# First pair's q and k loaded as f32 by SyncE and cast on chip; batch 0's masks added by VectorE

## The chip, the cores and the metric

The kernel runs on one core of a Trainium2 chip. The metric is the device time of one execution in microseconds (us), the median of several runs. Engines: PE (TensorE, matmuls), DVE (VectorE), ACT (ScalarE), POOL (GpSimd) and SP (SyncE, which here only issues DMAs). Each engine works through its own instruction list in order, and they wait for each other through semaphores.

## The reference

Sliding-window causal attention for 8 batches of 8 heads, 576 positions, head size 64, window 64; its output, as 4608 tokens of 512 features, goes through a two-layer network with the activation h cos(h).

```python
scores = scale * np.matmul(q, k.transpose(0, 1, 3, 2))      # scale = 1 / 8
rel = pos[:, None] - pos[None, :]
scores = np.where((rel >= 0) & (rel < 64), scores, -1000000000.0)
scores = scores - np.max(scores, axis=-1, keepdims=True)
attn = np.exp(scores)
attn = attn / (np.sum(attn, axis=-1, keepdims=True) + 1e-09)
x = np.matmul(attn, v)                       # then (B, H, S, D) -> (B*S, H*D)
h = x @ w_in                                 # 512 -> 2048
out = (h * np.cos(h)) @ w_out                # 2048 -> 512
```

## The kernel before, in words

**Units and groups.** A unit is 64 query positions of one batch and of one pair of heads, with the 128 key positions that they can see. Its scores are a tile of 128 x 128: 64 queries of each of the two heads on the partitions, 128 keys along the row. Four units make a group, which fills one PSUM bank (128 x 512 f32). Batch 0's first eight query blocks of the four pairs make eight groups, called (pair).(half) below; they are handled ahead of everything else.

**The first stage.** The string FIRST writes out the order of the first stage by hand. Each step emits the instructions of one piece of work, and as each engine works in order, the string sets the order on all of them. The steps: tq and tk transpose a pair's q and k on PE (18 transposes of 64 x 64 each, L186) into PSUM; pq and pk copy the result to SBUF, on DVE (d) or ACT (a); mk makes the masks; s is a group's scores on PE; m its maximum; e its four exponentials with their sums on ACT (L288); i the reciprocals on DVE; n the normalization (L302) on POOL (p) or DVE; w transposes the result on PE (L311) and c copies it; z spreads values of v; v is the product with the values on PE (L330), x its copy into xT; l issues the next weight or batch-1 load on POOL; tb loads ACT's sine table; h are the first matmuls of the first layer (L351). Behind the string the first token tile's dense matmuls run (L351, then L522), and batch 1's attention is placed between them by a list of due times, counted in groups of dense matmuls of PE.

**Loads.** All loads from memory are issued by POOL, which converts f32 to bf16 in the transfer: a pair of batch 0 (load_heads, 128 x 576) q and k apart, pair 0 first, then pairs 1, 2 and 3, the values, the weights and batch 1. The first issue on POOL stands behind the making of the identity matrix (masks.py), and the number ramp for the masks (iota, L115) stands behind the first two. SP issues nothing before 45 us.

**Masks.** From the ramp five DVE operations (L119 to L123) make three 128 x 128 f32 masks: 0 where a key may be seen, about -8e9 where not. Three ACT casts (L125) make a bf16 copy in the order that a group needs.

**Scores of batch 0** (g_scores). One matmul with the identity as weights writes a group's masks into the bank (L238, 128 x 512), and eight matmuls of 64 x 64 x 128 add the scores (L244). q had been multiplied by the scale when it was copied (L197, L199). g_max then takes the negated maximum of each of the four units with one reduction on DVE (L273), and the exponentials read the scores straight from PSUM.

**Scores of later batches** (burst). No mask matmul; for each unit one DVE operation (L277) adds the mask to the scores, multiplies by minus the scale, writes the result s to SBUF and yields the minimum of each row as the exponential's bias; a second instruction reads that minimum out. The exponentials read s, with scale -1.

Of the kernel before, what the change touches and what calls it, by code (L numbers as in the profile page):

```python
# [22 lines left out]
BIG = 3.0e38  # L23
# [28 lines left out]
def kernel(  # L52
# [34 lines left out]
    mask = const.tile([128, 3, 128], F32, name="mask")  # L87
    mask16 = const.tile([128, 6, 128], BF16, name="mask16")

# [28 lines left out]
    def put_masks():  # L118
        nc.vector.tensor_tensor(out=mask[:, 2], in0=mask[:, 0], in1=mask[:, 0], op=ALU.mult)  # L119
        nc.vector.tensor_scalar(mask[:, 1], mask[:, 2], 64.0 ** 2, NEG, ALU.is_gt, ALU.mult)  # L120
        nc.vector.tensor_scalar(mask[:, 2], mask[:, 1], -1.0, NEG, ALU.mult, ALU.add)
        nc.vector.tensor_copy(mask[:, 0, 0:64], mask[:, 2, 0:64])
        nc.vector.memset(mask[:, 0, 64:128], NEG)  # L123
        for lo, hi, of in ((0, 3, 0), (3, 5, 1), (5, 6, 1)):
            nc.scalar.copy(mask16[:, lo:hi], mask[:, of:of + hi - lo])  # L125

# [64 lines left out]
    def put(name, b, p, engine=None):  # L191
        of = st.pop(("t" + name, b, p)).rearrange("d (c p) -> d p c", c=RC)
        to = halves(turned(b))[name][:, p].rearrange("d (p c) -> d p c", c=RC)
        if b or name == "k":
            copy(engine, to, of)
        elif engine == "a":
            nc.scalar.mul(to, of, scale)  # L197
        else:
            nc.vector.tensor_scalar(to, of, scale, None, ALU.mult)  # L199

# [32 lines left out]
    def g_scores(n, which):  # L233
        s_ps = bank(S_FIRST[which], "s_ps")
        units = groups[n]
        s_ps = s_ps[:, 0:len(units) * 128].rearrange("p (u c) -> p u c", c=128)
        m0 = 2 if units[0][2] else 0
        nc.tensor.matmul(out=s_ps.rearrange("p u c -> p (u c)"), lhsT=ident,  # L238
                         rhs=mask16[:, m0:m0 + len(units)].rearrange("p u c -> p (u c)"),
                         start=True, stop=False, skip_group_check=True)  # L240
        for u, (b, p, j) in enumerate(units):
            for h in range(2):
                d = slice(64 * h, 64 * h + 64)
                nc.tensor.matmul(out=s_ps[d, u].rearrange("p (a t) -> p a t", a=2), lhsT=q_cols(b, p, j)[d],  # L244
                                 rhs=k_cols(b, p, j)[d], start=False, stop=u == len(units) - 1, skip_group_check=True)
        st["s", n] = s_ps
# [22 lines left out]
    def g_max(n):  # L269
        s_ps, units = st["s", n], groups[n]  # L270
        negm = att.tile([128, GF], F32, tag="negm", name="negm", bufs=8)
        if n < n_first:
            nc.vector.tensor_reduce(out=negm[:, 0:len(units)], in_=s_ps, op=ALU.max, axis=AX.X, negate=True)  # L273
        else:
            s = att.tile([128, GF, 128], F32, tag="s", name="s", bufs=4)
            for u, (b, p, j) in enumerate(units):
                nc.vector.tensor_tensor_reduce(out=s[:, u], in0=s_ps[:, u], in1=mask[:, 2 - j % 2 if j else 0],  # L277
                                               scale=-scale if b else -1.0, scalar=BIG, op0=ALU.add, op1=ALU.min,
                                               accum_out=negm[:, u:u + 1])
            st["s", n] = s  # L280
        st["m", n] = negm

    def g_exp(n):
# [3 lines left out]
        for u in range(len(groups[n])):  # L287
            nc.scalar.activation(e[:, u], s[:, u], AF.Exp, bias=negm[:, u:u + 1], scale=1.0 if n < n_first else -1.0,  # L288
                                 accum_out=den[:, u:u + 1])
# [157 lines left out]
    nc.vector.memset(small, 0.0)  # L447
    exp_table()
    make_identity(nc, ident)
    load_heads("q", 0, 0, 1)  # L450
    load_heads("k", 0, 0, 1)
    put_steps()
    for p0, n in ((1, 1), (2, 1), (3, 1)):
        for name in ("q", "k"):
            load_heads(name, 0, p0, n)
# [109 lines left out]
```

## Time and profile before

| what | us |
|---|---|
| runs: median of 3 (lowest to highest) | 307.88 (307.68 to 308.02) |
| profiled execution | 308.04 |
| its span, first to last instruction | 306.0 |
| busy PE / DVE / ACT / POOL | 294.1 / 219.3 / 235.6 / 171.9 |

The profile comes from one execution; its span leaves out some 2 us of the device time around the program. A timeline row gives the start in us, the duration, engine, line, operation, output<-input with shapes, and in brackets how long the engine was idle before it and what ended that. A row of the chain of waits gives start, duration and what the end of the program was then waiting for. A row of DMA issues gives the size of each and the median time from issue to landing. Rows by stretch give, after the stretch and its length, the busy time and instruction count of PE, its weight loads, DVE, ACT and POOL, then the clock that the TensorE was granted, the share of the DMA engines and GB/s.

### The profile page before, as it was taken

The numbers are of one execution on the slowest core, as the hardware profiler recorded it, in microseconds if no ns is written. First come the engines' busy times: TensorE is split into PE (matmuls) and PEld (weight loads), VectorE is DVE, ScalarE is ACT, GpSimd is POOL, SyncE is SP. The second block draws the span as 40 slices with busy tenths as digits, with TensorE's granted clock in tenths as the row PEclk, the third lists the DMA queues.
The fourth block names the chain that finished last, engine by engine and source line by source line (L and its number), as shares of the span: only waits on it lengthen the run. The fifth ranks groups of instructions, "written<-read, shape, count | busy, mean of one in ns | idle before, by whom it ended". The sixth has DMA issues, their size and how long they took to land.

```text
span 306.0 us, 7884 instructions
## 1 busy us (share of the span) xinstructions
PE 294.1 (96%) x2668; PEld 143.1 (47%) x2668; DVE 219.3 (72%) x832; ACT 235.6 (77%) x786; POOL 171.9 (56%) x200
## 2 busy tenths in 40 slices
PE   3979999999999999999999999999999999999996
PEld 2645444444444444444454445444544454454443
DVE  2796889678787778777878787788778877235701
ACT  4798689977997799879986998699869987106600
POOL 8997237889465976497759765957533630000000
PEclk9989999999999999999999999999999999999999
DMA  6999999599969999999999999999993441011012
GB/s 83 167 211 207 208 168 161 79 179 166 238 110 159 180 197 135 164 149 219 145 170 161 213 141 170 161 216 120 171 170 117 88 130 61 0 72 70 0 69 71
DMA packets 165577, 43.58 MB, mean 142 GB/s; under 512 B 154720, under 2 KB 161056, under 8 KB 165536
## 3 DMA queue, kind: packets, MB, share of 16 engines
q0 software_dynamic: 99632, 18.36, 75.4%
q1 hardware_dynamic: 65760, 24.52, 39.9%
q8 instruction: 21, 0.34, 0.5%
q10 hardware_dynamic: 144, 0.20, 0.2%
q14 instruction: 20, 0.16, 0.2%
HBM read 36.70 MB, written 9.44 MB: 151 GB/s over the span
## 4 chain that ended last, share of the span: by engine, by line
PE 83%; ACT 5%; DVE 5%; DMA 3%; POOL 1%; issue 1%; POOLq 0%; DVEq 0%
PE h_ps L351 41%; PE out_ps L522 33%; ACT e L288 3%; PE o_ps L330 3%; PE s_ps L261 3%; DMA rows<-in_q_dram 1%; PE out_ps L366 1%; DVE s L277 1%; DMA wT<-w 1%; DVE negm L273 1%; DVE w L302 1%; ACT L343 1%; PE tk_ps L186 1%; PE tq_ps L186 1%; POOL w L302 1%
## 5 line engine op out<-in xcount | busy, mean ns | idle before, releaser
L351 PE MATMUL h_ps<-xT,w_in 128*128 128x512 bf16 x576 | 128.1, 381 | 0.9 <-ACT xT L109 0.5
L522 PE MATMUL out_ps<-w_out,gT 128*128 128x512 bf16 x560 | 125.1, 379 | 0.2 <-DVE gT L510 0.2
L510 DVE TENSOR_TENSOR gT<-h_ps,sin 128x512 bf16<-128x512 f32 x144 | 95.5, 689 | 35.4 <-ACT sin L507 35.2
L507 ACT ACTIVATE sin<-h_ps 128x512 f32<-128x512 f32 x144 | 83.0, 599 | 34.2 <-PE h_ps L351 33.0
L288 ACT ACTIVATE e<-s,negm 128x128 f32<-128x128 f32 x256 | 98.6, 387 | 0.3 <-DVE negm L277 0.3
L302 POOL TENSOR_TENSOR w<-e,rden 128x512 bf16<-128x512 f32 (+1 forms) x76 | 74.3, 992 | 32.4 <-DVE rden L295 30.3
L351 PEld LDWEIGHTS <-w_in 128*128 128x128 bf16 x576 | 55.9, 98 | 66.7 <-issue 2.0
L522 PEld LDWEIGHTS <-gT 128*128 128x128 bf16 x560 | 53.2, 98 | 62.4 <-issue 0.2
L277 DVE CUSTOM_DVE_ANT_0 s<-s_ps,mask 128x128 f32<-128x128 f32 x256 | 58.1, 285 | 0.4 <-PE s_ps L261 0.4
L288 ACT ACTIVATION_READ_ACCUMULATOR e<-s,negm 128x1 f32 x256 | 48.0, 188 | 0.0
L149 POOL DMA_DIRECT2D rows<-in_q_dram x30 | 25.4, 866 | 25.3 <-DMA T<-rows 15.5
L162 POOL DMA_DIRECT2D v<-in_v_dram x35 | 29.6, 869 | 12.4 <-DMA rows<-in_k_dram 5.8
L109 ACT COPY out_sb<-out_ps 128x512 f32<-128x512 f32 (+1 forms) x18 | 10.1, 561 | 24.4 <-PE out_ps L522 19.0
L295 DVE RECIPROCAL rden<-den 128x4 f32<-128x4 f32 (+1 forms) x80 | 13.8, 172 | 18.3 <-ACT e L288 17.1
L149 POOL DMA_DIRECT2D rows<-in_k_dram x30 | 25.5, 898 | 0.5 <-DMA T<-rows 0.5
L109 DVE CAST xT<-o_ps 128x512 bf16<-128x512 f32 x26 | 16.9, 681 | 6.5 <-PE o_ps L330 6.2
L277 DVE DVE_READ_ACCUMULATOR2_ANT negm<- 128x1 f32 x256 | 21.3, 83 | 0.0
L109 DVE COPY out_sb<-out_ps 128x512 f32<-128x512 f32 x18 | 12.4, 689 | 12.0 <-PE out_ps L522 12.0
L288 ACT ACTIVATE e<-s_ps,negm 128x128 f32<-128x128 f32 x32 | 11.4, 394 | 1.6 <-DVE negm L273 1.4
L261 PE MATMUL s_ps<-T 64*64 64x128 bf16 x512 | 12.1, 221 | 0.0
L261 PEld LDWEIGHTS <-T 64*64 64x64 bf16 x512 | 8.2, 106 | 8.3 <-DVE negm L277 3.9
L330 PEld LDWEIGHTS <-v 128*64 128x64 bf16 x504 | 9.7, 114 | 4.4 <-issue 2.3
(54 smaller groups left out, 148.9 us busy)
## 6 DMA issues: line engine op xcount, KB each, us to landing
out_dram<-out_sb SPq DMA_DIRECT2D x16, 512.0 KB, 6.9
v<-in_v_dram POOLq DMA_DIRECT2D x28, 128.0 KB, 8.3
rows<-in_q_dram POOLq DMA_DIRECT2D x24, 128.0 KB, 5.9
rows<-in_k_dram POOLq DMA_DIRECT2D x24, 128.0 KB, 9.0
w_out<-in_moe_w_out_dram POOLq DMA_DIRECT2D x2, 1024.0 KB, 16.8
w_in<-in_moe_w_in_dram POOLq DMA_DIRECT2D x2, 768.0 KB, 12.1
wT<-w SPq DMA_TRANSPOSE x66, 3.8
out_dram<-out_sb SPq DMA_DIRECT2D x3, 256.0 KB, 2.0
```

The source lines that it names most:

```text
L109: {"a": nc.scalar.copy, "p": nc.gpsimd.tensor_copy}.get(engine, nc.vector.tensor_copy)(out, in_)
L149: nc.gpsimd.dma_start(out=rows(b)[lo:lo + n, slot * 512:slot * 512 + 512].rearrange("p (h d) -> p h d", h=H), in_={"q": q, "k": k}[name][b ...
L162: nc.gpsimd.dma_start(out=vt.rearrange("p (h d) -> p h d", h=H), in_=v[b, :, c * 128:c * 128 + n, :].rearrange("h p d -> p h d"))
L261: nc.tensor.matmul(out=s_ps[cross][to, u].rearrange("p (a t) -> p a t", a=2), lhsT=q_cols(b, p, j)[d], rhs=k_cols(b, p, j)[d], start=True, ...
L277: nc.vector.tensor_tensor_reduce(out=s[:, u], in0=s_ps[:, u], in1=mask[:, 2 - j % 2 if j else 0], scale=-scale if b else -1.0, scalar=BIG, ...
L288: nc.scalar.activation(e[:, u], s[:, u], AF.Exp, bias=negm[:, u:u + 1], scale=1.0 if n < n_first else -1.0, accum_out=den[:, u:u + 1])
L302: (nc.gpsimd if engine == "p" else nc.vector).tensor_tensor(out=w[:, 0:u], in0=e[:, 0:u], op=ALU.mult, in1=rden[:, 0:u].unsqueeze(2).to_br ...
L330: nc.tensor.matmul(out=o_ps[64 * h:64 * h + 64, 64 * i:64 * i + 64], lhsT=values_of(b)[:, max(j - 1, 0), 128 * p + 64 * h:128 * p + 64 * h ...
L351: nc.tensor.matmul(out=st["h", ff], lhsT=w_in_sb[:, ks, ff * 128:ff * 128 + 128], rhs=st["xT", mt][:, ks], start=start, stop=stop)
L507: nc.scalar.activation(sin, h_ps, AF.Sin, bias=math.pi / 2.0)
L510: nc.vector.tensor_tensor(out=gt[:, e], in0=h_ps, in1=sin, op=ALU.mult)
L522: nc.tensor.matmul(out=o_ps[e], lhsT=gT[ff // 2][:, ff % 2, ms * 128:ms * 128 + 128], rhs=w_out_sb[:, ff], start=ff == 0, stop=ff == n_ff - 1)
```

## The change

Pair 0's q and k of batch 0 are loaded by SP as f32 into two buffers of the output pool, one behind the other, ahead of anything else that the program issues; ACT casts q and DVE casts k into the place where POOL's loads put them before. POOL's first two loads are now pair 1's. Batch 0's groups lose the mask matmul and take the masked minimum of later batches (L277 before, L262 in the change); the scale goes into that operation for all batches, and the exponentials read s from SBUF with scale -1. The bf16 masks and their three casts are gone, and the pool of s has 8 buffers instead of 4.

```diff
-    mask16 = const.tile([128, 6, 128], BF16, name="mask16")
...
-        for lo, hi, of in ((0, 3, 0), (3, 5, 1), (5, 6, 1)):
-            nc.scalar.copy(mask16[:, lo:hi], mask[:, of:of + hi - lo])
...
-        if b or name == "k":
-            copy(engine, to, of)
-        elif engine == "a":
-            nc.scalar.mul(to, of, scale)
-        else:
-            nc.vector.tensor_scalar(to, of, scale, None, ALU.mult)
+        copy(engine, to, of)
...
-        m0 = 2 if units[0][2] else 0
-        nc.tensor.matmul(out=s_ps.rearrange("p u c -> p (u c)"), lhsT=ident,
-                         rhs=mask16[:, m0:m0 + len(units)].rearrange("p u c -> p (u c)"),
-                         start=True, stop=False, skip_group_check=True)
...
-                                 rhs=k_cols(b, p, j)[d], start=False, stop=u == len(units) - 1, skip_group_check=True)
+                                 rhs=k_cols(b, p, j)[d], start=True, stop=True, skip_group_check=True)
...
-        if n < n_first:
-            nc.vector.tensor_reduce(out=negm[:, 0:len(units)], in_=s_ps, op=ALU.max, axis=AX.X, negate=True)
-        else:
-            s = att.tile([128, GF, 128], F32, tag="s", name="s", bufs=4)
-            for u, (b, p, j) in enumerate(units):
-                nc.vector.tensor_tensor_reduce(out=s[:, u], in0=s_ps[:, u], in1=mask[:, 2 - j % 2 if j else 0],
-                                               scale=-scale if b else -1.0, scalar=BIG, op0=ALU.add, op1=ALU.min,
-                                               accum_out=negm[:, u:u + 1])
-            st["s", n] = s
+        s = att.tile([128, GF, 128], F32, tag="s", name="s", bufs=8)
+        for u, (b, p, j) in enumerate(units):
+            nc.vector.tensor_tensor_reduce(out=s[:, u], in0=s_ps[:, u], in1=mask[:, 2 - j % 2 if j else 0],
+                                           scale=-scale, scalar=BIG, op0=ALU.add, op1=ALU.min,
+                                           accum_out=negm[:, u:u + 1])
+        st["s", n] = s
...
-            nc.scalar.activation(e[:, u], s[:, u], AF.Exp, bias=negm[:, u:u + 1], scale=1.0 if n < n_first else -1.0,
+            nc.scalar.activation(e[:, u], s[:, u], AF.Exp, bias=negm[:, u:u + 1], scale=-1.0,
...
+    first_f32 = {}
+    for name, src in (("q", q), ("k", k)):
+        first_f32[name] = moe.tile([128, 2, d_model], F32, tag="out", name="first_f32", bufs=3).rearrange("p a b -> p (a b)")[:, 0:S]
+        nc.sync.dma_start(out=first_f32[name], in_=src[0, 0:2].rearrange("h (p c) d -> (h p) (c d)", c=RC))
     make_identity(nc, ident)
-    load_heads("q", 0, 0, 1)
-    load_heads("k", 0, 0, 1)
+    load_heads("q", 0, 1, 1)
+    load_heads("k", 0, 1, 1)
     put_steps()
-    for p0, n in ((1, 1), (2, 1), (3, 1)):
+    for name, engine in (("q", "a"), ("k", "d")):
+        copy(engine, halves(rows(0))[name][:, 0], first_f32[name])
+    for p0, n in ((2, 1), (3, 1)):
```

The order on two engines shows what the change moves at the start. On DVE before, from the program's first instruction to the first group's maximum (L119 to L123 are the masks, tq_ps the transposed q, T its copy, s_ps the scores):

```order
L447 MEMSET small 128x1
L119 TENSOR_TENSOR mask<-mask 128x128 [waits Pool_49]
L120 TENSOR_SCALAR mask<-mask 128x128 [waits DVE_49]
L121 TENSOR_SCALAR mask<-mask 128x128 [waits DVE_49]
L122 COPY mask<-mask 128x64 [waits DVE_49]
L123 MEMSET mask 128x64
L199 TENSOR_SCALAR T<-tq_ps 128x576 [waits PE_49]
L273 TENSOR_REDUCE negm<-s_ps 128x4 [waits PE_49]
```

The same place of the change (rows_72 is the tile of batch 0's q and k, first_f_86 the f32 buffer of k):

```order
L432 MEMSET small 128x1
L108 CAST rows_72<-first_f_86 128x576 [waits DMAHW1_49]
L118 TENSOR_TENSOR mask<-mask 128x128 [waits Pool_49]
L119 TENSOR_SCALAR mask<-mask 128x128 [waits DVE_49]
L120 TENSOR_SCALAR mask<-mask 128x128 [waits DVE_49]
L121 COPY mask<-mask 128x64 [waits DVE_49]
L122 MEMSET mask 128x64
L108 COPY T<-tq_ps 128x576 [waits PE_49]
L262 ISA s,negm<-s_ps,mask 128x128 [waits PE_49]
L262 ISA negm 128x1
```

The cast of k, which waits for SP's second load, stands ahead of the five mask operations, which stood first; and a group's one reduction has become four pairs of masked minimum and readout, of which the first is shown. On ACT before, from the table load to the third pair's q and on to the first group of pair 2:

```order
L343 ACT_TABLE_LOAD
L343 ACTIVATE small<-small 128x1
L125 CAST mask_81<-mask 128x384
L125 CAST mask_81<-mask 128x256
L125 CAST mask_81<-mask 128x128
L109 COPY T<-tk_ps 128x576
L288 ACTIVATE e,den<-s_ps,negm 128x128 x4
L197 ACTIVATE T<-tq_ps 128x576
L288 ACTIVATE e,den<-s_ps,negm 128x128 x12
```

And in the change:

```order
L328 ACT_TABLE_LOAD
L328 ACTIVATE small<-small 128x1
L108 CAST rows_72<-first_f_84 128x576
L108 COPY T<-tk_ps 128x576
L273 ACTIVATE e,den<-s,negm 128x128 x4
L108 COPY T<-tq_ps 128x576
L273 ACTIVATE e,den<-s,negm 128x128 x12
```

The cast of q stands where the three mask casts stood, and the exponentials read s in place of the PSUM bank.

## The prediction

> **What bounds the kernel now.** I read first the busy time of two stretches of the span: up to the point where the dense matmuls of the first token tile begin, and behind it. Columns: stretch, length, then busy time and instructions of PE, PE's weight loads, DVE, ACT and POOL.
>
> ```profile
> 0.00:26.21 26.21, 18.42 (x318) 12.29 (x319) 17.08 (x37) 19.35 (x79) 25.04 (x37) 0.93 1.18 160
> 26.21:306.00 279.79, 275.73 (x2350) 130.77 (x2349) 202.18 (x795) 216.22 (x708) 146.87 (x164) 1.00 1.16 141
> ```
>
> Behind 26.2 us PE is busy 275.7 of 279.8 us. Everything there follows PE's program, and the change touches no instruction of it. So the question is only how far the start of the dense part moves. In the first 26.2 us POOL is busy 25.0, and ACT 19.4 although it starts late: no single engine bounds that stage; several run in step.
>
> Next the chain of waits in that stretch (start, length, what):
>
> ```profile
> 1.45 1.29 POOL rows L142 x2
> 3.25 4.54 DMA rows<-in_q_dram
> 9.26 0.54 PE s_ps L238
> 10.37 0.48 PE tq_ps L186 x18
> 13.58 0.69 DVE negm L273
> 15.66 0.93 DVE w L302
> 24.19 1.28 ACT L346
> 26.21 0.81 PE h_ps L351 x3
> ```
>
> The reader is to see three parts: a wait for the second pair's q rows, which POOL issues third (3.25 to 7.79 us); then PE, with a mask matmul exposed between transposes; from 13.6 us on DVE, and at the end ACT's table load. Every part meets an edit.
>
> **The first pair's start.** Timeline rows of the first pair, with its load issues:
>
> ```profile
> 1.45 0.74 POOL L142 DMA_DIRECT2D rows<-in_q_dram  x1
> 3.33 0.29 DVE L119 TENSOR_TENSOR mask<-mask 128x128 f32<-128x128 f32 x1 [2.46 <-POOL mask L115]
> 4.54 1.02 ACT L125 CAST mask<-mask 128x384 bf16<-128x384 f32 x3 [2.30 <-DVE mask L123]
> 4.82 0.69 PE L186 MATMUL tq_ps<-ident,rows 64*64 64x64 bf16 x18 [4.82 <-DMA rows<-in_q_dram]
> 5.55 0.76 DVE L199 TENSOR_SCALAR T<-tq_ps 128x576 bf16<-128x576 bf16 x1 [1.10 <-PE tq_ps L186]
> 6.22 0.64 ACT L109 COPY T<-tk_ps 128x576 bf16<-128x576 bf16 x1 [0.66 <-PE tk_ps L186]
> 6.91 0.63 PE L244 MATMUL s_ps<-T 64*64 64x128 bf16 x8 [0.19 <-ACT T L109]
> out_dram<-out_sb SPq DMA_DIRECT2D x16, 512.0 KB, 6.9
> out_dram<-out_sb SPq DMA_DIRECT2D x3, 256.0 KB, 2.0
> out_dram<-out_sb ACTq DMA_DIRECT2D x1, 192.0 KB, 1.9
> ```
>
> No f32 load through SP stands in this trace. The nearest rows are SP's and ACT's own transfers: 192 KB lands 1.9 us behind its issue and 256 KB 2.0 us, on nearly idle DMA engines; 512 KB under load takes 6.9. Each new load is 128x576 f32, 288 KB. The engines are idle until POOL's first load moves, so I take 2.3 us for q. SP is free once the others are, near 0.75 us (ACT's and POOL's first instructions start at 0.74), so q lands at 3.05 and k, issued behind it on the same queue, at 3.7. The upper bound is POOL's price: 3.37 us (1.45 to 4.82) for a load with half the bytes, so q at 4.1 and k at 4.75; the lower is 1.9 us, so q at 2.65.
>
> The Trainium skill (DMA: Bandwidth & Descriptors, Anatomy of one DMA) gives some 2.0 us fixed plus the bytes at 436 GB/s, which makes 2.7 us an estimate for q. By that sum q lands at 3.45, and the gain at this place is 0.4 us smaller; the trace's 256 KB in 2.0 us is quicker than the page's sum.
>
> The q cast on ACT takes 0.65 us (a 128x576 copy takes 0.64), so pair 0's transposes start at 3.75 instead of 4.82. For the k cast on DVE no row stands: it lies between 0.29 (the 128x128 f32 mask operation) and 0.76 (128x576 from PSUM), and cannot be free; I take 0.5, halfway. It stands **ahead of the mask operations**, which wait behind it: DVE is through them 1.12 us later (3.33 to 4.45 now; ACT's cast, which waits for the last, starts at 4.54), at 3.7 + 0.5 + 1.12 = 5.3. The put of q on DVE therefore starts at 5.3, though its transposes are done at 4.45, and the first scores start near 6.1 instead of 6.91: **0.8 us earlier**. ACT's three mask casts (1.02 us) were hidden under the load and bring nothing.
>
> **The second pair and the mask matmuls.** PE's rows at the two clocks, and POOL's issues:
>
> ```profile
> 7.83 0.69 PE L186 MATMUL tq_ps<-ident,rows 64*64 64x64 bf16 x18 [0.29 <-DMA rows<-in_q_dram]
> 12.37 0.61 PE L238 MATMUL s_ps<-mask,ident 128*128 128x512 bf16 x1
> 13.76 0.39 PE L238 MATMUL s_ps<-mask,ident 128*128 128x512 bf16 x1
> 19.51 0.40 PE L311 MATMUL tw_ps<-ident,w 128*128 128x128 bf16 x4 [1.48 <-POOL w L302]
> 5.35 0.58 POOL L142 DMA_DIRECT2D rows<-in_q_dram  x1
> 5.87 0.59 POOL L142 DMA_DIRECT2D rows<-in_k_dram  x1
> 11.67 1.04 POOL L302 TENSOR_TENSOR w<-e,rden 128x512 bf16<-128x512 f32 x1
> ```
>
> Pair 1's q is now POOL's first issue and lands near 4.8, long before PE is through the first scores (6.1 and their 0.63, some 0.2 of it overlapped by the next transposes). PE goes straight on at 6.55 instead of 7.83: 1.3 us. Behind pair 1's two transposes (0.7 + 0.65) one mask matmul is gone (0.54 of the chain), so the third pair's q transposes start near 8.25 instead of 10.16, and ACT's copy of them near 8.95 instead of 10.88: **1.9 us**. The other mask matmuls lie where PE waits for others anyway.
>
> **What takes it back.** Rows of the new operations where batch 1 runs them already, of the operations that they replace, and the spread of the DVE one:
>
> ```profile
> 43.41 0.39 ACT L288 ACTIVATE e<-s,negm 128x128 f32<-128x128 f32 x1
> 43.80 0.39 ACT L288 ACTIVATE e<-s,negm 128x128 f32<-128x128 f32 x1
> 11.43 0.36 ACT L288 ACTIVATE e<-s_ps,negm 128x128 f32<-128x128 f32 x1
> 11.77 0.37 ACT L288 ACTIVATE e<-s_ps,negm 128x128 f32<-128x128 f32 x1
> 20.45 0.47 ACT L288 ACTIVATE e<-s_ps,negm 128x128 f32<-128x128 f32 x1
> 21.13 0.37 ACT L288 ACTIVATE e<-s_ps,negm 128x128 f32<-128x128 f32 x1
> 42.63 0.28 DVE L277 CUSTOM_DVE_ANT_0 s<-s_ps,mask 128x128 f32<-128x128 f32 x1
> 42.84 0.29 DVE L277 CUSTOM_DVE_ANT_0 s<-s_ps,mask 128x128 f32<-128x128 f32 x1
> L277 DVE CUSTOM_DVE_ANT_0 s<-s_ps,mask x256: 258/286/293, 42.6 to 243.2; 128x128 f32<-128x128 f32 x128
> L273 DVE TENSOR_REDUCE negm<-s_ps 128x4 f32<-128x512 f32 x8 | 5.4, 678 | 2.7 <-PE s_ps L244 2.7
> ```
>
> An exponential that reads SBUF starts 0.385 us behind the one before it (43.41 to 43.80), one that reads PSUM 0.345: 28 of them behind the third pair's copy cost ACT 28 x 0.04 = 1.1 us. One masked minimum follows the other by 0.21 us, so a group of four takes 0.85 where the reduction takes about 0.6 (0.68 busy, 0.08 overlapped by what follows): seven groups behind the first cost DVE 7 x 0.25 = 1.7 us. The 256 instances lie within 0.258 to 0.293 us although POOL works beside many of them, so I add nothing for contention.
>
> So ACT's 1.9 us shrink to 0.8 plus the idle time that it loses: the last group's exponentials start 0.68 us behind the group before (20.45 to 21.13), 0.33 over the pitch, a wait for DVE that falls away if DVE comes earlier. That makes about **1.1**. DVE's 1.9 less 1.7 is 0.2 by sums; but of the 2.7 us that it idles ahead of its reductions for PE's scores, only 1.3 lie ahead of the first group (5.55 + 0.76 to 6.91 + 0.63), and the other 1.4 are filled by scores that come sooner: 1.0 to 1.5, about 1.2.
>
> POOL is the third engine of the step. Its issues lie 0.52 us apart (5.35 to 5.87) and it works back to back up to 24 us; SP takes two loads off it, **1.04 us**. PE waits 1.48 us for one of its products at 19.51, so without this the other gains would end there.
>
> All three engines thus reach the tail (last exponentials, last product, table load, last xT) 1.0 to 1.2 us earlier; I take **1.1**. The profiled execution lasts 308.04 us with a span of 306.0; it becomes 306.9. It stands 0.16 above the median of the runs, 307.88, so the predicted median is **306.8**.
>
> **The rivals.**
>
> 1. *The dense matmuls start at half clock: slower.* The columns are as in the first view; the seventh is the granted clock.
>
> ```profile
> 10.16:13.57 3.41, 3.41 (x71) 2.41 (x68) 2.05 (x3) 2.69 (x14) 3.35 (x5) 1.00 2.10 163
> 16.98:20.40 3.42, 1.94 (x43) 1.27 (x41) 3.42 (x9) 3.42 (x20) 3.34 (x3) 0.98 1.18 215
> 20.40:23.81 3.41, 3.16 (x33) 1.87 (x28) 3.00 (x7) 2.82 (x14) 3.39 (x5) 0.52 1.15 208
> ```
>
> After a stretch of 3.4 us with PE busy throughout, the mask matmul fell from 0.61 to 0.39 us; after one with 1.94 of 3.42 busy the clock was 0.52 for the next 3.4 us, and full again behind one with 3.16. The change takes eight mask matmuls out. If the stretch ahead of the dense part no longer counts as busy, that part starts at half clock: each such stretch does half its work and costs 1.7 us, and a prologue at half clock throughout gives back about 0.6 of the gain besides: 306.8 + 1.7 + 0.6 = 309.1. It decides where PE's busy share of the last 3.4 us ahead of the dense part falls well below 3.16; PE keeps every transpose, value and h matmul there, and I work out about 2.9 to 3.1. Chance 0.18. By the Trainium skill (TensorE: Matmul & The Clock Gate, Part 1: The HAM clock gate) the gate watches free-running windows of 3413 ns and is at half rate unless the last was busy. The trace agrees on the 3.4 us; no run so far shows another phase of the window.
>
> 2. *The loads land late.* SP's pair at POOL's price (q 4.1, k 4.75), or shared with POOL's loads: DVE reaches the put at 4.75 + 0.5 + 1.12 = 6.4, later than now (5.55), the scores start at 7.15, 0.25 late. What pair 1 gains (0.3 of DMA wait, 0.54) is then all: 307.8. For it: SP's 512 KB under load take 6.9 us, 3.9 for 288 KB in proportion; against: nothing else moves before POOL's first load does. Chance 0.17.
>
> 3. *More.* PE keeps the full clock through 20 to 24 us, and the h, transposing and value matmuls there shorten by about 0.6: 306.2. Chance 0.10.
>
> 4. *DVE becomes the bound:* masked minimum and readout do not overlap, 0.29 + 0.08 each, 1.48 a group, 0.88 more in seven groups, 6.2 against 1.9 gained with 1.4 of idle: 2.9 late, 311. The pitch of 0.21 in batch 1 speaks against it. Chance 0.04.
>
> 5. *Nothing arrives:* the dense part starts early but then waits for a transfer. The rows show PE waiting for none behind 26 us, and POOL's loads move ahead with it: 307.8. Chance 0.06.
>
> **How the numbers follow.** Forecast 0.45, the rivals 0.18, 0.17, 0.10, 0.04 and 0.06. A measurement of this kernel can tell about 0.2%, 0.6 us, from no change. The forecast's own range is 306.2 to 307.5 (q's landing 2.65 to 3.6); nine tenths of it and rival 3 are faster: 0.50, and 0.04 of rival 2: 0.54. Within: the rest of the forecast and of 2, and 5: 0.05 + 0.09 + 0.06 = 0.20. Slower: 1, 4 and the tail of 2: 0.26. The range from 305.9 to 308.8 holds all but the worse half of rival 1, rival 4 and the ends.
>
> **What would show it.** In the profile after: q's cast on ACT near 3.05 and k's on DVE near 3.7; first scores near 6.1; second pair's q transposes with no DMA wait near 6.55; third pair's copy near 8.95; POOL's first product near 10.6 instead of 11.67; exponentials 0.385 apart; first long run of h matmuls near 25.1 at full clock. Casts behind 4.5 us make rival 2 right, a granted clock near 0.5 behind 25 us rival 1, and a prologue that ends early with an unchanged end rival 5.

## The result, and the profile after

| | before | after |
|---|---|---|
| median (lowest to highest), 9 runs each | 308.07 us (307.68 to 308.78) | 307.12 us (306.67 to 308.15) |
| ratio, 95% interval | | 0.9972 (0.9961 to 0.9982) |
| profiled execution / its span | 308.04 / 306.0 | 306.92 / 305.0 |
| dense part starts (in the profile) | 26.21 | 25.76 |
| from there to the end of the span | 279.79 | 279.24 |

The change gains 0.28%, 0.95 us by the medians, 1.1 us by the two profiled executions. But only 0.45 us of that is an earlier dense start, where the forecast had all of it; the other half came behind it.

The beginning of the first stage after, from the timeline and the DMA issues (columns as in the prediction's rows):

```profile
first_f<-in_q_dram SPq DMA_DIRECT2D x1, 288.0 KB, 2.9
first_f<-in_k_dram SPq DMA_DIRECT2D x1, 288.0 KB, 3.1
3.68 0.67 ACT L108 CAST rows<-first_f 128x576 bf16<-128x576 f32 x1 [1.44 <-DMA first_f<-in_q_dram]
4.37 0.46 DVE L108 CAST rows<-first_f 128x576 bf16<-128x576 f32 x1 [3.49 <-DMA first_f<-in_k_dram]
5.77 0.70 DVE L108 COPY T<-tq_ps 128x576 bf16<-128x576 bf16 x1
6.52 0.64 PE L232 MATMUL s_ps<-T 64*64 64x128 bf16 x8 [0.94 <-DVE T L108]
6.95 0.69 PE L183 MATMUL tq_ps<-ident,rows 64*64 64x64 bf16 x18
9.27 0.64 ACT L108 COPY T<-tq_ps 128x576 bf16<-128x576 bf16 x1
20.05 0.39 ACT L273 ACTIVATE e<-s,negm 128x128 f32<-128x128 f32 x1
```

The loads take 2.9 and 3.1 us from issue to landing. The first scores start 0.39 us earlier than before, the second pair's q transposes 0.88, ACT's copy of the third pair's q 1.61, and the last group's exponentials 1.08 (21.13 before). So about 1.1 us does reach the last exponentials. POOL's first product, at 11.67 before, starts at 10.56, and POOL is not idle ahead of it: it has two issues fewer to make. Then the end of the first stage, PE with the DVE and ACT rows that bear on it, before and after:

```profile
19.51 0.40 PE L311 MATMUL tw_ps<-ident,w 128*128 128x128 bf16 x4 [1.48 <-POOL w L302]
19.84 1.05 PE L330 MATMUL o_ps<-wT,v 128*64 128x64 bf16 x32
20.37 0.66 DVE L273 TENSOR_REDUCE negm<-s_ps 128x4 f32<-128x512 f32 x1
20.83 0.61 PE L311 MATMUL tw_ps<-ident,w 128*128 128x128 bf16 x4
20.95 0.68 DVE L109 CAST xT<-o_ps 128x512 bf16<-128x512 f32 x1
21.68 1.44 PE L351 MATMUL h_ps<-xT,w_in 128*128 128x512 bf16 x3 [0.25 <-DVE xT L109]
23.59 0.58 ACT L109 COPY wT<-tw_ps 128x512 bf16<-128x512 bf16 x1 [0.48 <-PE tw_ps L311]
```

```profile
18.60 0.61 PE L296 MATMUL tw_ps<-ident,w 128*128 128x128 bf16 x4 [1.49 <-POOL w L287]
19.14 1.06 PE L315 MATMUL o_ps<-wT,v 128*64 128x64 bf16 x32
20.14 0.61 PE L296 MATMUL tw_ps<-ident,w 128*128 128x128 bf16 x4
20.28 0.29 DVE L262 CUSTOM_DVE_ANT_0 s<-s_ps,mask 128x128 f32<-128x128 f32 x1
20.49 0.69 DVE L108 CAST xT<-o_ps 128x512 bf16<-128x512 f32 x1
21.23 1.44 PE L336 MATMUL h_ps<-xT,w_in 128*128 128x512 bf16 x3 [0.48 <-DVE xT L108]
23.13 0.58 ACT L108 COPY wT<-tw_ps 128x512 bf16<-128x512 bf16 x1 [0.97 <-PE tw_ps L296]
25.76 0.59 PE L336 MATMUL h_ps<-xT,w_in 128*128 128x512 bf16 x2 [0.38 <-ACT xT L108]
```

At the transposes that wait for POOL's product the gain is still 0.91 us; at the first h matmuls it is 0.45, and it stays there to the dense start. Two things lie between. Four transposes take 0.61 us instead of 0.40: PE runs at half clock there. And the first h matmul waits for DVE's cast to xT, which stands behind the last group's maximum: before, the cast starts 0.06 us behind the end of the products with v (19.84 + 1.05); after, the four masked minima of that group keep DVE until 20.49, 0.29 us behind that end (19.14 + 1.06). These are 0.21 and 0.23 us, nearly all of the 0.46 that is lost. From the first h matmul to the dense start both kernels take 4.53 us, with PE at half clock for the first 2 us or so, and ACT's gain ends in waiting there: 0.97 us for PE's transposes instead of 0.48.

In the profile before PE was at full clock from 13.4 to 20.3 us; in the one after, the transposes and scores take the longer of their two times from the start, four transposes 0.61 to 0.64 us up to 22.5 us, so in this execution the clock does not rise until the stage is nearly over.

Behind the dense start, POOL's second product of batch 1, before and then after:

```profile
49.93 0.82 POOL L302 TENSOR_TENSOR w<-e,rden 128x384 bf16<-128x384 f32 x1 [1.21 <-PE s_ps L261]
51.31 0.83 POOL L302 TENSOR_TENSOR w<-e,rden 128x384 bf16<-128x384 f32 x1 [0.56 <-DVE negm L277]
```

```profile
49.47 0.82 POOL L287 TENSOR_TENSOR w<-e,rden 128x384 bf16<-128x384 f32 x1 [1.50 <-PE s_ps L249]
50.49 0.82 POOL L287 TENSOR_TENSOR w<-e,rden 128x384 bf16<-128x384 f32 x1 [0.20 <-DVE rden L280]
```

The first product is 0.46 us earlier, like everything; the second 0.82. PE waited for it before (0.18 us of idle time at 52.19) and does not now. That is 0.36 us that the prediction has no term for.

### The profile page after: what moved, and what is told of

Its sections match the earlier page's. It is cut to its first block, busy times and chain, and to the rows that moved or that the text cites. A ratio compares the mean times of both kernels' runs of the same rounds, so it can differ in the third digit from the quotient of the medians.

```text
span 305.0 us, 7899 instructions
## 1 busy us (share of the span) xinstructions
PE 292.1 (96%) x2660; PEld 143.6 (47%) x2660; DVE 219.9 (72%) x889; ACT 236.1 (77%) x784; POOL 170.7 (56%) x198
## 4 chain that ended last, share of the span: by engine, by line
PE 83%; DVE 6%; ACT 6%; DMA 2%; issue 1%; POOL 1%; SPq 0%; DVEq 0%; POOLq 0%
PE h_ps L336 41%; PE out_ps L513 33%; ACT e L273 3%; PE o_ps L315 3%; PE s_ps L249 3%; DVE s L262 3%; PE out_ps L351 1%; DMA wT<-w 1%; DMA first_f<-in_k_dram 1%; DVE T L108 1%; POOL w L287 1%; DVE w L287 1%; ACT L328 1%; PE tw_ps L296 1%; DVE wT L108 0%
## 5 line engine op out<-in xcount | busy, mean ns | idle before, releaser
L273 ACT ACTIVATE e<-s,negm 128x128 f32<-128x128 f32 x288 | 111.0, 388 | 1.6 <-DVE negm L262 1.6
L262 DVE CUSTOM_DVE_ANT_0 s<-s_ps,mask 128x128 f32<-128x128 f32 x288 | 64.9, 283 | 0.9 <-PE s_ps L232 0.7
L273 ACT ACTIVATION_READ_ACCUMULATOR e<-s,negm 128x1 f32 x288 | 54.1, 188 | 0.0
L146 POOL DMA_DIRECT2D rows<-in_q_dram x30 | 25.4, 867 | 26.8 <-DMA T<-rows 17.4
L262 DVE DVE_READ_ACCUMULATOR2_ANT negm<- 128x1 f32 x288 | 23.9, 83 | 0.0
L315 PE MATMUL o_ps<-wT,v 128*64 128x64 bf16 x504 | 11.5, 200 | 0.1
```

The costliest lines, as they stand in the source:

```text
L146: nc.gpsimd.dma_start(out=rows(b)[lo:lo + n, slot * 512:slot * 512 + 512].rearrange("p (h d) -> p h d", h=H), in_={"q": q, "k": k}[name][b ...
L315: nc.tensor.matmul(out=o_ps[64 * h:64 * h + 64, 64 * i:64 * i + 64], lhsT=values_of(b)[:, max(j - 1, 0), 128 * p + 64 * h:128 * p + 64 * h ...
```

## The experiments

Each kernel is given as its difference to the kernel before or to the change, with cut code marked by three dots. The kernel before, timed beside them, had medians of 307.9 to 308.05 us, and the ratios are to that. Each profile is of one execution.

**The two halves of the change alone.** *Loads alone*: the kernel before with the new loads and casts, and nothing of the masks.

```diff
...
+        nc.sync.dma_start(out=first_f32[name], in_=src[0, 0:2].rearrange("h (p c) d -> (h p) (c d)", c=RC))
...
-    load_heads("q", 0, 0, 1)
-    load_heads("k", 0, 0, 1)
+    load_heads("q", 0, 1, 1)
+    load_heads("k", 0, 1, 1)
...
+        copy(engine, halves(rows(0))[name][:, 0], first_f32[name])
```

> The kernel before with the f32 loads through SP and their casts alone; mask matmuls, reductions and exponentials from PSUM stay. Theory (the loads bring the gain, and the mask part gives some of it back, chiefly by leaving PE so idle that the clock stays at half through the first 23.5 us): PE is kept busy by the mask matmuls, the clock rises within the first 16 us as before, the dense matmuls start near 25.2 us (26.21 before, 25.76 after), time near 307.1 or below. Rival (the gain comes from the mask matmuls that fall away): dense start not before 25.9, time near 307.9.

*Masks alone*: the change with these lines put back as they were.

> The change without the f32 loads: all pairs through POOL as before, no mask matmul, masked minimum on DVE, exponentials from SBUF. Theory: the first scores start at 6.9 as before, 0.5 us of mask matmul falls away, DVE has 1.7 us and ACT 1.1 us more to do, and PE's clock stays at half up to about 23 us: dense start near 26.8, time 308.5 to 309.0. Rival (the mask part pays by itself): dense start near 25.8, time near 307.4.

Measured: loads alone 306.65 us, ratio 0.9961 (0.9943 to 0.9979); masks alone 309.17 us, ratio 1.0030 (1.0019 to 1.0042). The loads make the gain, by the medians all of it and more (the intervals of the loads alone and of the change overlap); the masked minimum on DVE costs 1.1 us where the loads come late (in its profile, 308.71 us, the dense part starts at 26.54, 0.33 later than before). The half clock that both theories counted on did not come as they had it: in the profile of the masks alone the matmuls are at full clock from 10.9 to 17.8 us. The profile of the loads alone is of an execution of 308.18 us, 1.5 above its median, with its dense start at 27.20 instead of the 25.2 expected; the reason stands under *Two queues*. The two numbers do not add up to the change (306.65 and 1.1 make 307.75 against 307.12), so the halves interact. One place where they meet stands in the timeline of the loads alone:

```profile
5.90 1.02 ACT L125 CAST mask<-mask 128x384 bf16<-128x384 f32 x3 [1.59 <-DVE mask L123]
6.96 0.59 PE L238 MATMUL s_ps<-mask,ident 128*128 128x512 bf16 x1 [1.44 <-ACT mask L125]
```

DVE's mask operations stand behind the k cast, ACT's mask casts behind them, and the mask matmul waits 1.44 us for these. The change takes that wait away with the mask matmul; another order takes it away too.

**The order.** *Loads with the masks first*: loads alone, with the mask operations ahead of the k cast on DVE. *Change with the masks first*: the same in the change. In both the step mk is gone from FIRST.

```diff
-    for name, engine in (("q", "a"), ("k", "d")):
-        copy(engine, halves(rows(0))[name][:, 0], first_f32[name])
+    copy("a", halves(rows(0))["q"][:, 0], first_f32["q"])
+    put_masks()
+    copy("d", halves(rows(0))["k"][:, 0], first_f32["k"])
```

> The kernel before with the f32 loads and casts alone (mask matmuls, reductions and exponentials from PSUM kept), and the mask operations and their ACT casts placed ahead of the k cast. Theory A (the gain is the loads', the masked minimum costs time): ACT's mask casts end near 5.6 instead of near 6.9, the first scores start near 6.3, and the time falls below that of the loads alone (306.65) by 0.2 to 0.5: 306.1 to 306.5. Theory B (the mask half of the change is needed to use the early loads): not faster than the loads alone, 306.6 to 307.1.

> The change with one thing moved: the cast of k on DVE stands behind the five mask operations instead of ahead of them. Theory A (the price of that order was small once the loads landed at 3.65 and 4.35 us): masks 3.3 to 4.45, k cast 4.45 to 4.95, first scores near 6.35 instead of 6.52, and then the third pair's rows (0.24 us of wait at 8.54 now) take what is left: 306.9 to 307.2. Theory B (the order is what the change pays most for, as the forecast counted it with 1.12 us ahead of the first scores): first scores near 5.9, third pair's q transposes 0.4 or more earlier, 306.4 to 306.7.

Measured: loads with the masks first 306.46 us (305.84 to 306.94), ratio 0.9953 (0.9939 to 0.9966); change with the masks first 306.90 us, ratio 0.9970 (0.9959 to 0.9980). Two rows of each, the first of loads with the masks first:

```profile
4.54 1.02 ACT L125 CAST mask<-mask 128x384 bf16<-128x384 f32 x3
6.36 0.64 PE L244 MATMUL s_ps<-T 64*64 64x128 bf16 x8 [0.16 <-ACT T L109]
```

```profile
6.34 0.63 PE L232 MATMUL s_ps<-T 64*64 64x128 bf16 x8 [0.73 <-ACT T L108]
8.54 0.69 PE L183 MATMUL tq_ps<-ident,rows 64*64 64x64 bf16 x18
```

Theory A held in both. With this order the scores start at the same 6.35 us with and without a mask matmul, and the kernel that keeps the mask matmuls is 0.44 us faster by the medians. In the change itself the order is worth 0.2 us by the medians, which the ratios (0.9972 and 0.9970) do not tell from nothing: the first scores gain 0.18, and the third pair's q transposes start at 8.54 as they did, so the gain ends there. With early loads the masked minimum costs 0.47 us in the one order and 0.44 in the other, against 1.1 with late loads; so the wait for the mask casts is not what makes the halves interact, and what does is not shown.

*The first pair's masks alone on DVE*: loads with the masks first, and groups 0 and 1 without mask matmul, as in the change.

```diff
...
-        nc.tensor.matmul(out=s_ps.rearrange("p u c -> p (u c)"), lhsT=ident,
+        if n > 1:
+            nc.tensor.matmul(out=s_ps.rearrange("p u c -> p (u c)"), lhsT=ident,
...
-        if n < n_first:
+        if 2 <= n < n_first:
...
```

> The same kernel, and the first pair's two groups alone without mask matmul, with the masked minimum on DVE; the other six groups of batch 0 keep matmul, reduction and exponentials from PSUM. Theory A (a mask matmul costs 0.54 us of PE where it is exposed, and only the first pair's second one is; the masked minimum costs DVE 0.25 a group): within 0.3 us of the loads with masks first, 306.0 to 306.6. Theory B (the mask matmuls of the first pair were what held the first stage): 305.4 to 305.9.

Measured: 306.53 us, ratio 0.9956 (0.9939 to 0.9973), within the 0.3 us that theory A gave, but the runs spread from 305.58 to 308.51. The profiled execution lasts 307.59, 1.1 above that median and 0.7 us longer than the change's, though its dense part starts at 25.08, 0.7 us ahead of the change. So in this execution something behind the dense start takes more than the earlier start brings.

**The end of the first stage.** The profiles so far, with two that follow, part the two terms of the 0.46 us. From the four transposes that wait for POOL's product to the first h matmul it is (start of each in brackets):

| | full clock | half clock |
|---|---|---|
| one reduction for the last group | 2.17 us (loads with masks first: 18.44, 20.61) | 2.38 us (first pair's masks on DVE: 18.17, 20.55) |
| four masked minima | 2.42 us (*warm*, below: 18.37, 20.79) | 2.63 us (change: 18.60, 21.23) |

The clock costs 0.21 us and the masked minima cost 0.25, the first in both rows, the second in both columns; the kernel before took 2.17 (19.51, 21.68).

**PE's clock.** *Warm*: the change with idle matmuls and transposes of the identity in PE's gaps, so that the clock stays up: WARM ahead of the first transposes, FILL ahead of a group's scores, FILL_W ahead of its transposes.

```diff
...
+WARM = 28
+FILL = {1: 7, 2: 2, 4: 4}
+FILL_W = {0: 10, 2: 4, 3: 18}
...
+        for _ in range(FILL.get(n, 0)):
+            nc.tensor.matmul(out=s_ps[:, 0], lhsT=ident, rhs=ident, start=True, stop=True, skip_group_check=True)
...
+            for _ in range(FILL_W.get(n, 0)):
+                nc.tensor.transpose(t_ps[:, 0], ident, ident)
...
+    warm = bank("O0", "warm_ps")
+    for _ in range(WARM):
+        nc.tensor.matmul(out=warm[:, 0:128], lhsT=ident, rhs=ident, start=True, stop=True, skip_group_check=True)
...
```

> The change with 41 idle matmuls of 128x128 (identity by identity) and 32 transposes of the identity in PE's gaps of the first stage, into banks that are overwritten afterwards; the results are unchanged. Theory (the half clock costs the change about 0.6 us): the clock is full from about 8 us, transposes of 18 take 0.47 instead of 0.69 us, the dense matmuls start near 25.1 instead of 25.76, time near 306.5. Rival (PE's speed lies beside DVE, ACT and POOL and costs nothing): dense start 25.7 to 25.9, time 307.1.

Measured: 307.81 us, ratio 0.9982 (0.9969 to 0.9996). At full clock from 4.4 us on, the dense part started at 24.52, **1.24 us earlier** than in the change: that is what half clock throughout the first stage costs. But 0.80 of it lies behind the first h matmul (3.73 us from there to the dense start against 4.53), where the kernel before is at half clock too and takes the same 4.53. The time expected, 306.5, did not come: the end of the profile was 1.0 us *later* than the change's. PE's timeline behind the dense start:

```profile
57.53 0.32 PE L322 MATMUL o_ps<-wT,v 128*64 128x64 bf16 x8 [0.34 <-DMA wT<-w]
61.24 0.41 PE L322 MATMUL o_ps<-wT,v 128*64 128x64 bf16 x14 [0.77 <-DMA wT<-w]
91.32 0.51 PE L322 MATMUL o_ps<-wT,v 128*64 128x64 bf16 x20 [0.30 <-DMA wT<-w]
122.70 0.47 PE L322 MATMUL o_ps<-wT,v 128*64 128x64 bf16 x18 [0.38 <-DMA wT<-w]
```

Four waits, 1.8 us, for SP's transposing transfers of the normalized scores; the change's profile has none of them. From the dense start to the end this kernel takes 2.24 us longer than the change, and these waits are most of it. These transfers landed 3.5 us behind their issue in the change (median of 66) and 4.6 here. The clock's price is shown; why the transfers are slower in this kernel is not.

*Four buffers*: the change with `bufs=4` for s, as before.

> The change with 4 buffers for s, as before, instead of 8. Theory (the half microsecond that the change's profile gains behind the dense start, between 50 and 53 us, is no effect of the buffers): same dense start, same time, 307.1 within 0.3. Rival (more buffers let DVE run ahead in batch 1): about 0.5 us slower, 307.6, with DVE waiting for ACT between 42 and 60 us.

Measured: 307.12 us, ratio 0.9968 (0.9957 to 0.9978), dense start 25.75: the number of buffers plays no role. This profile also shows that the clock does not follow from the kernel alone. Its first stage has the same instructions as the change's; a row of it and the same place of the change:

```profile
10.63 0.47 PE L183 MATMUL tq_ps<-ident,rows 64*64 64x64 bf16 x18
```

```profile
10.80 0.73 PE L183 MATMUL tq_ps<-ident,rows 64*64 64x64 bf16 x18
```

Here the matmuls are at full clock from 10.4 to 17.2 us, as they are in the change with the masks first from 10.2 and with the masks alone from 10.9, sooner than before (13.4); none of the three has a mask matmul in batch 0. So taking out the mask matmuls does not by itself keep the clock down. And the full clock between 10.4 and 17.2 us brought nothing at the dense start: what the two profiles share is half clock from 17.2 to 23.5 us.

**What takes the early start.** In the profile of the kernel with the first pair's masks on DVE, PE's longest wait behind the dense start is for batch 2's q and k (T, transposed by SP from the rows that POOL loads); two waits of 0.2 us follow near 183 and 215. Its row, and the summary of that tile in the change:

```profile
74.50 0.64 PE L262 MATMUL s_ps<-T 64*64 64x128 bf16 x32 [0.95 <-DMA T<-rows]
```

```profile
L249 PE MATMUL s_ps<-T x32: 216/216/240, 74.2 to 74.6; 64*64 64x128 bf16 x32
L150 SPq DMA_TRANSPOSE T<-rows x2: 3938/4199/4460, 58.4 to 65.6; - x2
DMA to landing us min/median/max: 8.3/8.5/8.8
```

In the change SP issues the second transfer at 65.6 us and it lands 8.3 us later, at 73.9; PE reads it from 74.16 on. The slack is 0.25 us, and no wait shows. Three kernels move POOL's loads of batch 2's last k chunks, on which SP's issue waits; each is the kernel with the first pair's masks on DVE and one due time changed (load_chunk for k, b = 2): both chunks two of POOL's products earlier, one of them two products earlier, or one ahead of all eight products.

```diff
...
-            at(t0 - T + ((19.4 if c < 2 else 28.6) + 0.01 * c if b == 2 else 10.5 + 0.9 * c) if c < 4 else
+            at(t0 - T + ((19.4 if c < 2 else 27.3) + 0.01 * c if b == 2 else 10.5 + 0.9 * c) if c < 4 else
...
```

```diff
...
+            at(t0 - T + ((19.4 if c < 2 else 27.3 if c == 2 else 28.6) + 0.01 * c if b == 2 else 10.5 + 0.9 * c) if c < 4 else
...
```

```diff
...
+            at(t0 - T + ((19.4 if c < 3 else 28.6) + 0.01 * c if b == 2 else 10.5 + 0.9 * c) if c < 4 else
...
```

> The kernel with early loads, masks first and the first pair's masks on DVE, whose dense part starts at 25.08 us, with one thing moved: POOL issues batch 2's last two k chunks two products earlier (near 54.6 instead of 56.7). Theory A (what eats the earlier start is batch 2's rows: chunks issued by POOL, landing, then SP's transposing transfer, 0.95 us late for PE at 74.5): the transfer lands about 2 us earlier, PE waits no longer at 74, the executions at 307 and above disappear, median 305.7 to 306.2; the two products behind the chunks come 1.1 us later and may cost up to 0.4. Theory B (the early start is lost for another reason, and the wait only shows it): the median stays at 306.4 to 306.8 and the spread as it was (305.6 to 308.5).

> The same with one chunk of the two moved. Theory A: the last chunk is issued some 0.5 us earlier, products are 0.4 us later; half of the wait at 74 goes, median 305.9 to 306.4. Theory B: 306.4 to 306.8.

> The kernel with early loads, masks first and the first pair's masks on DVE, with batch 2's third k chunk issued by POOL ahead of batch 1's eight products, where POOL idles some 1.4 us, so that the last chunk goes out one issue (0.9 us) earlier and no product waits for it. Theory A (batch 2's rows hold the early start back): no wait for the transposed rows near 74, no wait for POOL's products near 56, dense part at 24.5 to 25.4 by the phase of the clock, median 305.6 to 306.3. Theory B (something else behind the dense start takes it): 306.4 to 306.9, as without it.

Measured, in this order: 306.95 us (306.63 to 308.23), ratio 0.9972 (0.9959 to 0.9985); 306.57 us (305.48 to 307.31), ratio 0.9951 (0.9932 to 0.9970); 306.64 us (306.57 to 306.99), ratio 0.9964 (0.9951 to 0.9978). The wait near 74 us is gone in all three profiles, and in the first and the third the runs lie closer together. But no median fell below 306.5: theory A was right on the wait and wrong that the time would follow. A row of the first and one of the third show what came in its place:

```profile
56.50 0.34 PE L312 MATMUL tw_ps<-ident,w 128*128 128x128 bf16 x3 [0.88 <-POOL w L303]
```

```profile
51.21 0.34 PE L312 MATMUL tw_ps<-ident,w 128*128 128x128 bf16 x3 [0.18 <-POOL w L303]
```

In the first, POOL's products stand 1.8 us of load issues later and PE waits 0.88 us for one of them (0.4 was expected). In the third, the late second product that the kernel before has came back. The profile of the second, an execution of 307.31 us, takes 280.0 us from its dense start at 25.41 and shows no wait of this size; where it loses its time is open. From the dense start at 24.48 the first takes 280.2 us to the end, where loads with the masks first take 279.1 from 25.45: there the earlier start ran into the next product. The four kernels of this family have the same first stage, and their profiles start the dense part at 25.08, 24.48, 25.41 and 25.22 us, the first of the three at full clock from 11.4 us to the end of the stage; so a difference of some tenths between two dense starts can be the execution and not the edit.

**Two queues.** The change with the masks first, and k's load issued on ACT's queue ahead of its table load. It was run twice, the second time for one more profiled execution.

```diff
...
-    exp_table()
     first_f32 = {}
...
-        nc.sync.dma_start(out=first_f32[name], in_=src[0, 0:2].rearrange("h (p c) d -> (h p) (c d)", c=RC))
+        {"q": nc.sync, "k": nc.scalar}[name].dma_start(out=first_f32[name], in_=src[0, 0:2].rearrange("h (p c) d -> (h p) (c d)", c=RC))
+    exp_table()
...
```

> The change with k's load issued on ACT's queue ahead of its table load, beside q's on SP's, and the k cast behind the mask operations. Theory A (2.9 us of a load is latency, the 0.7 us between q and k is SP's second issue behind the first, and the engines have room): q lands at 3.65 as before, k at 3.7 to 3.9. Theory B (the bytes set it): both land near 4.0 to 4.4. Either way the time stays within 0.3 us of the kernel with SP alone and the k cast behind the masks, since the third pair's rows limit: 306.8 to 307.2.

> The change with k's load on ACT's queue once more, for a profile of one of its slower executions (nine of twelve lay at 307.5 to 308.8, the profiled one at 306.75 with its dense start at 25.47). Theory A (batch 2's rows): a wait of PE for the transposed rows near 74 us of 0.5 us or more. Theory B (the first pair's loads scatter): q and k land 1 us later than in the first profile (4.5 and 4.6), and the dense part starts near 26.5.

Measured: 308.29 us, ratio 1.0002 (0.9989 to 1.0016); the profiled execution of the first lasted 306.75, of the second 308.32. The time, expected at 306.8 to 307.2, was wrong under both theories. On the loads theory B came near: side by side they take 3.7 (q) and 3.9 us (k) and are cast from 4.50 and 4.67, so q comes 0.8 us later than on one queue and k no sooner.

The later q tells what the early loads are worth. Rows of the first profile:

```profile
7.12 0.63 PE L232 MATMUL s_ps<-T 64*64 64x128 bf16 x8 [0.73 <-ACT T L108]
10.47 1.04 POOL L287 TENSOR_TENSOR w<-e,rden 128x512 bf16<-128x512 f32 x1
18.48 0.40 PE L296 MATMUL tw_ps<-ident,w 128*128 128x128 bf16 x4 [1.85 <-POOL w L287]
```

The first scores start 0.78 us later than in the change with the masks first (6.34), later even than in the kernel before (6.91). But POOL's first product is not later (10.47 against 10.60, and 11.67 before), nor the transposes that wait for POOL near 18.4 us (18.48 against 18.44). The third kernel with a chunk moved says the same: scores at 7.16, product at 10.48. So what the loads through SP bring up to those transposes is, in these profiles, that POOL has two issues fewer, and not that the first pair's scores come sooner. What the second pair's rows add, which POOL now issues first, no run parts from this.

The dense part starts at 25.47 us in the first profile and at 27.13 in the second. The difference begins here, at DVE's normalization of group (1).(0) and POOL's copy of values, first in the execution of 306.75 us and then in that of 308.32:

```profile
14.87 0.69 DVE L287 TENSOR_TENSOR w<-e,rden 128x512 bf16<-128x512 f32 x1
14.89 2.42 POOL L108 COPY v<-v 64x2048 bf16<-64x2048 bf16 x1
```

```profile
15.10 2.27 DVE L287 TENSOR_TENSOR w<-e,rden 128x512 bf16<-128x512 f32 x1
14.94 1.89 POOL L108 COPY v<-v 64x2048 bf16<-64x2048 bf16 x1
```

Where DVE starts 0.02 us ahead of POOL it takes 0.69 us and POOL's copy 2.42 instead of 1.89; where POOL starts first, DVE takes 2.27 us, to 0.54 us behind POOL's end. The same stands in the profile of the loads alone (DVE 15.34, 2.40 us; POOL 15.30, 1.89), an execution of 308.18 us beside a median of 306.65. In the execution of 308.32 us PE is also at half clock from 15.4 to 25.7 us, in that of 306.75 from 20.4 to 23.8, so the collision need not be the whole difference. Both theories of the second run fell: PE does not wait for batch 2's rows, and the loads come within 0.25 us of the first profile's (cast from 4.74 and 4.56). In the change DVE starts at 14.27 and POOL's copy, which waits 0.62 us for its values, at 15.54: out of each other's way by 0.06 us (DVE ends at 15.48).

## Why the prediction came out

The time was right, 306.92 for the profiled execution against 306.9, and so was the direction: the f32 loads let the first stage run ahead, and the masked minimum takes part of that back. By the medians 307.12 stands against 306.8, with a gain of 0.95 against 1.1. But that the number fits so well is luck: it is the sum of two errors that cancel.

- **The loads.** 2.3 us each was too little: 2.9 and 3.1. q's cast starts at 3.68 instead of 3.05, the first scores at 6.52 instead of 6.1. The bounds (1.9 and 3.37 us) held both. The rows that I preferred are of stores to memory, not of loads. The Trainium skill's sum (DMA: Bandwidth & Descriptors, Anatomy of one DMA), an estimate of 2.7 us, was nearer, though the page gives it for DMAs that GpSimd issues. What the loads save before the first scores did not decide: with these 0.78 us later, POOL's products and the transposes that wait for them came as early. The term that counted is POOL's two issues, 1.04 us in the forecast and 1.11 at its first product (10.56), 0.91 at the transposes that wait for POOL.
- **The k cast ahead of the masks**: its own 0.46 us was forecast as 0.5, and from its start to the put of q the timeline has 1.4 us where the forecast had 1.6. Yet masks first gain only 0.18 at the scores, since k lands at 4.35, when the mask operations would just be done.
- **Second and third pair.** 0.88 instead of 1.3 us and 1.61 instead of 1.9: the late loads, and a wait of 0.24 us for the third pair's rows at 8.54 that the step "PE goes straight on" did not have.
- **What takes it back.** ACT's 1.1 us came as worked out: exponentials 0.385 apart, the last group 1.08 us earlier. The masked minima follow each other by 0.21 us. DVE's term was counted for all seven groups together; that the last group's minima stand straight ahead of the cast that PE waits for was not in it. In the change's profile POOL waits 0.62 us for the values (15.54), which the forecast did not see; with four buffers there is no such wait, and POOL's copy ends at the same 17.4 us, since it takes 2.18 us instead of 1.89.
- **The dense start, 25.76 instead of 25.1: the first error.** The step that failed is "All three engines thus reach the tail ... 1.0 to 1.2 us earlier", which leaves PE out of the sum. ACT's last exponentials did come 1.08 us earlier and POOL's product let PE start 0.91 us earlier, but the first h matmul came only 0.45 earlier: 0.21 us went to transposes at half clock, priced at the clock of the profile before, and 0.25 to the masked minima ahead of the cast to xT. From there to ACT's last copies PE, at half clock before and after, sets the pace, and ACT waits for it. The "0.6 of the gain" for a slow first stage stood in rival 1, as a side cost of a slow dense part; 0.21 of it came without that. The dense part started at full clock, but not for the reason given: the stretches 6.40 to 9.82 and 9.82 to 13.23 us of the change's profile, with 3.01 us of PE busy in each, were followed by half clock, the one from 20.06 to 23.47 with 2.92 by full clock. So a busy time near 3 us does not tell what follows.
- **Behind the dense start: the second error.** "Everything there follows PE's program" held for the change to within the 0.55 us by which that stretch became shorter, 0.36 of it at one POOL product. That product is late in the profiles before, of the masks alone and of the kernel with one chunk ahead of all products, and in time in the others; what decides it is not settled.
- **Rival 5** was put at 0.06 because PE waits for no transfer behind 26 us. The experiments show that this was the wrong thing to read: in one profile each, 0.7 us more of an early start met a wait of 0.95, and 1.24 us more met four waits of 1.8 together. An early start is not the only thing that decides: the profile of the loads alone, with its dense start 1.4 us later than the change's, still waits 0.2 us for batch 2's rows.

## What to carry to other kernels

A wait that is absent from a profile is not slack: before an earlier start is counted to the end, compare the landing of each transfer and the end of each product with the start of its reader (here 73.9 and 74.16 us). Run the halves of a change apart, and then each with the order that suits it: here the loads with the mask operations first beat the whole change by 0.66 us by the medians. Follow a gain to the engine that sets the pace at the end of the stage: here 1.1 us at ACT became 0.45 at PE, whose next operand stood behind DVE's new work. PE's clock in a short first stage differs from one execution to the next, so price its work there at both clocks.

## What was not expected of the hardware

- A DVE operation of 0.69 us took 2.27 and 2.40 us when a POOL copy had started 0.16 and 0.04 us ahead of it; with the order reversed POOL's copy took 2.42 instead of 1.89. The Trainium skill (SBUF — State Buffer, SBUF: two separate sides) says that DVE and GpSimd share a pair of ports as a lock, which the one that starts first holds for its whole instruction; for a DVE operation with two inputs in SBUF, as this one, it says so against a GpSimd operation that reads SBUF. The rows agree, and with them a shift of 0.18 us between the two starts stands beside 1.5 us of the kernel's time.
- Two loads of 288 KB on two queues took 3.7 and 3.9 us, on one queue 2.9 and 3.1 with 0.45 us between their issues: the second queue brought nothing here.
- Two executions with the same instructions in the first stage had the clock rise at 10.4 us (four buffers) and at 23.5 (the change). The stretch of 3.41 us ahead of the rise had PE busy for 2.98 us in the first; one with 3.01 in the second was followed by half clock.
- The clock column reads 1.00 through the first stage of the change, though the matmuls there take half-clock times (18 transposes 0.69 us against 0.47 at full clock); ahead of the first rise the durations tell more.
